# A list scheduler that follows two DMA rings, and packed attention scores unpacked by one wide and two corner masks

## The chip, the cores and the metric

The kernel runs on one NeuronCore of a Trainium2 chip. A core has a matrix engine (TensorE, "PE" in the profile; its weight loads are a row of their own, "PEld"), a vector engine (VectorE, "DVE"), an activation engine (ScalarE, "ACT"), GpSimd ("POOL") and SyncE ("SP"). Each engine runs its own instructions in their order and waits for the others through semaphores. Transfers are issued here from two queues, POOL's (loads, with a cast from float32 to bfloat16) and SP's (transposes and stores), and are carried by the core's 16 DMA engines. The metric is the device time of one execution in microseconds (us), less is better.

## The reference

Eight batches of eight heads, 576 positions, 64 numbers per head: sliding-window attention with a linear position bias, then a two-layer feed-forward network with squared ReLU on the 4608 tokens.

```python
scores = scale * np.matmul(q, k.transpose(0, 1, 3, 2))
rel = pos[:, None] - pos[None, :]
bias = slopes[:, None, None] * (-np.abs(rel).astype(np.float32))[None, :, :]
mask = (rel >= 0) & (rel < window)                 # window = 128
scores = np.where(mask, scores + bias[None], -1000000000.0)
attn = softmax(scores); attn_out = np.matmul(attn, v)
x = attn_out.transpose(0, 2, 1, 3).reshape(4608, 512)
out = np.maximum(x @ w_in, 0.0) ** 2 @ w_out       # w_in 512x2048, w_out 2048x512
```

## The kernel before

**Attention.** A batch is cut into five blocks of queries: four of 128 and one of 64, so there are 40 blocks, numbered m = 0 to 39 (called b0, b1 and so on in the order of loads). A block sees its own keys and those of the block before it. `load_block` loads k, q and v of a block; `turn` transposes k and q into `kqT`, on TensorE for the blocks of `KQ_PE`, else by a DMA transpose from SP (line 439); `score` issues the score matmuls; then come an exponential on ScalarE, a product on VectorE with a mask that holds bias and window, and in `mix` the product with v (line 612), whose extra column of ones gives the sum of the softmax, its reciprocal (635), the scaling (640), and the transpose of the result into `xT`, on TensorE for the blocks of `X_PE`, else by DMA (650).

**Packed scores.** From block 6 on, a whole block that is not the first of its batch is handled in "quarters". For a pair of heads the unpacked score row has 256 columns: 128 queries against the block's own keys, then the same 128 queries against the keys of the block before. Of those the lower 64 key rows can be non-zero in columns 0 to 191 only, and the upper 64 in columns 64 to 255 only. So the 64x64 parts of the array write 192 columns for each half of the keys (line 521), packed to the front of the bank; one exponential of 128x384 (two heads' pairs) reads them into `raw`, and two products of 64x384 (line 569, one for each half of the keys, because their columns start at different places) spread them into `Pq`. There are 21 such blocks, with four exponentials and eight products each. Score matmuls of three half blocks go out as one burst (`UNITS`), 48 matmuls where all are packed. Other blocks (line 530, 584, 591) are not packed; a 64-row block and the first block of the next batch form a pair.

**Feed-forward.** Tokens go in nine groups of 512 (g0 to g8). `fc_step` (line 716) makes 128 of the 2048 inner features for a group, `relu` and `square` follow on ScalarE (725) and VectorE (732), and `t_part` (778) multiplies four of 16 feature blocks into an output tile of 128 tokens. The group g+1 of the first layer is interleaved with the group g of the second. Group 0 is done in two halves of 256 tokens, group 1 in three parts (`SPLIT`). The weights come in four loads each, i0 to i3 (`w_in`) and o0 to o3 (`w_out`), between the first blocks, in the order of `FIRST`.

**Order.** `Plan` is a list scheduler that runs when the kernel is built. Every piece of work is a task with costs in ns per engine it may use, dependencies, buffers to take and to give back, and a key. `order` repeatedly takes the task that can start first; between tasks that can start at the same time the key decides. The key of attention work is a due time (`where`), less `AHEAD` or `LEAD`. The order that comes out is what the engines execute: a task whose data are later than planned holds up all that is behind it on its engine. A transfer is modelled by one number, `dma_free`: transfers go one after another, each with its own cost, whichever queue issued them. At most eight transfers are outstanding on a queue (`lanes`). `fill` puts matmuls on zeros ("filler", line 818) into planned gaps of TensorE before 26 us, and `warm` puts some at the very start.

Of the kernel before, what the change touches and what calls it, by code (L numbers as in the profile page):

```python
# [11 lines left out]
ALU = mybir.AluOpType  # L12
# [26 lines left out]
class Plan:  # L39


    LAT = {"PE": 260.0, "ACT": 220.0, "DVE": 220.0, "POOL": 200.0, "SP": 2200.0}
    BEGIN = {"POOL": 1260.0}

    def __init__(self, bufs, pools, cold, share):
        self.tasks = []
        self.bufs = bufs
        self.pools, self.cold, self.share = pools, cold, share
        self.bursts = []
        self.dma_free = 0.0  # L50

# [25 lines left out]

    def order(self):
        used = {tag: [] for tag in self.bufs}
# [17 lines left out]
        def avail(t):  # L97
            at = t.ready
            if t.dma is not None or t.engs.get("SP"):
                e = next(iter(t.engs))  # L100
                if len(lanes[e]) >= 8:
                    at = max(at, lanes[e][-8])
            more = {}
            for s in t.acq:
                if s.idx is not None:
                    continue
                more[s.tag] = more.get(s.tag, 0) + 1
                if s.tag in held:
                    if s.ffn:
                        at = self.ration(t, at, held[s.tag], left, used, free)  # L110
                        if at is None:
                            return None
                    free_at = sorted(0.0 if x is None else x.freed for x in held[s.tag] if x is None or not x.left)
                    if len(free_at) < more[s.tag]:
                        return None
                    at = max(at, free_at[more[s.tag] - 1])
                    continue
                u = used[s.tag]
                n = self.bufs[s.tag]
                i = len(u) + more[s.tag] - 1 - n  # L120
                if i >= 0:
                    old = u[i]
                    if old.left:
                        return None
                    at = max(at, old.freed)
            return at

        self.used = used
        done = []
        n_all = len(self.tasks)  # L130
        while len(done) < n_all:
            best = None
            for e, c in cand.items():
# [12 lines left out]
                if lo is not None and (best is None or lo[0][0] < best[0]):  # L146
                    best = (lo[0][0], e, lo[1])
            if best is None:
                raise RuntimeError("plan is stuck: " + repr([
# [7 lines left out]
            if t.dma is not None:  # L157
                at = max(st + dur + 900.0, self.dma_free)
                self.dma_free = at + t.dma
                t.end = self.dma_free + 900.0  # L160
                lanes[e].append(t.end)
            else:
                t.end = st + dur + (self.LAT[e] if t.lat is None else t.lat)
                if e == "SP":
                    lanes[e].append(t.end)
            free[e] = st + dur
            for x in t.engs:
                cand[x].remove(t)
            for s in t.acq:
# [11 lines left out]
                u.append(s)  # L181
            for s in t.rel:
                s.left -= 1
                s.freed = max(s.freed, t.end)
            for u in t.users:
                left[u] -= 1
                u.ready = max(u.ready, st + dur if e == "PE" and "PE" in u.engs else t.end)
                if not left[u]:
                    for x in u.engs:
                        cand[x].append(u)  # L190
            done.append(t)
# [5 lines left out]
def kernel(  # L197
# [17 lines left out]

    FIRST = "b0 b1 b2 b3 i0 i1 i2 o0 b4 b5 i3 o1 b6 b7 o2 b8 o3 b9"
    SPLIT = {0: [(0, 256), (256, 512)], 1: [(0, 192), (192, 320), (320, 512)]}
    EARLY = 0
    AHEAD = {10: -30, 1: 30, 4: 60, 9: -60, 5: 60, 0: 0, 12: 60, 11: 0, 2: -60, 8: -30, 7: 90, 6: 0, 3: 30, 24: 0, 14: 60, 18: 30, 25: 30, 23: 30, 16: -30, 13: 90, 21: 0, 19: 30, 17: 0, 22: 0, 20: 60, 15: 30}
    LEAD = 40  # L220

    KQ_PE = [0, 1, 2, 3, 4, 5, 6, 7, 8]
    X_PE = [0, 1, 2, 3, 4, 5, 6, 7, 8, 12, 17]
    WARM = 28
    FILL, UNTIL = 0.4, 26e3
    COLD = 12000
    QUARTERS = 6
    V0 = 1
    SHARE, SOON = 3, 500
    LONG, UNITS = 5, 3  # L230
    W_IN = [0, 4, 8, 12, 16]
    PAIR_AFTER, PAIR_KEY = 2, -140
    BANKS = {"A": 8}
# [21 lines left out]

    size = {"kq": 7, "v": 7, "kqT": 5, "P": 2, "x": 4, "Pq": 2, "raw": 2}
    kq = ring("kq", size["kq"], [128, 2, d_model])
    vt = ring("vt", size["v"], [128, H, D + 1])
    kqT = ring("kqT", size["kqT"], [128, 2 * C, 128])
    Pt = {nm: ring(nm, size[nm], [128, H, 2, 128]) for nm in ("P", "Pq")}  # L260
    raw = ring("raw", size["raw"], [128, H, 192])
    xt = ring("x", size["x"], [128, d_model])
# [92 lines left out]

    def load(key, ns, emit, deps=(), acq=()):
        return plan.add({"POOL": 900.0}, key, emit, deps, acq, dma=ns)

# [3 lines left out]
    def load_w_in(n, key):  # L362
        lo, hi = 128 * W_IN[n], 128 * W_IN[n + 1]

        def emit():
            nc.gpsimd.dma_start(w_in_sb[:, :, lo:hi], moe_w_in[:, lo:hi].rearrange("(c p) f -> p c f", p=128))  # L366
        t = load(key, {256: 1400.0, 512: 2550.0}[hi - lo], emit)
        t_win[W_IN[n]:W_IN[n + 1]] = [t] * (W_IN[n + 1] - W_IN[n])

    def load_w_out(n, key):  # L370
        def emit():
            nc.gpsimd.dma_start(
                w_out_sb[:, 4 * n:4 * n + 4, :],
                moe_w_out[n * 512:(n + 1) * 512, :].rearrange("(c p) f -> p c f", p=128))
        t_wout[n] = load(key, 2550.0, emit)

    s_in, t_in = {}, {}

    def load_block(m, key):
# [5 lines left out]
        for i, (nm, src) in enumerate((("k", k), ("q", q), ("v", v))):  # L385
            sl = s_in[m, nm]
            if wide and nm != "v":
                def emit32(i=i, src=src):
                    nc.sync.dma_start(kq32[:, i].rearrange("s (h d) -> s h d", h=H),
                                      src[b, :, kb * 128:kb * 128 + n, :].rearrange("h s d -> s h d"))  # L390
                t_in[m, nm] = plan.add({"SP": 450.0}, key + 0.01 * i, emit32, dma=870.0)
                continue
# [36 lines left out]
    def turn(m):  # L429
# [7 lines left out]
        if kq_by_dma:  # L437
            def turn_kq():
                nc.sync.dma_start_transpose(kqT[sk.idx], kq[s_in[m, "k"].idx].rearrange("s t f -> s (t f)"))
            t_kq = [plan.add({"SP": 1300.0}, due - 80, turn_kq, [t_in[m, "k"], t_in[m, "q"]], [sk],  # L440
                             [s_in[m, "k"]], dma=1300.0)]
        elif m == 0:
# [58 lines left out]
    def score(units):  # L501
# [8 lines left out]
        def burst():  # L510
            for sl in slots.values():
                bank(sl)
            for (ms, sP, work_of, _), j in units:
                for c in (2 * j, 2 * j + 1) if sP.tag == "Pq" else ():
                    m = ms[0]
                    for part, k0, q0, q1 in ((1, 0, 0, 128), (1, 64, 64, 128), (0, 64, 0, 128), (0, 0, 0, 64)):
                        mk = m - 1 + part
                        lo = (c % 2) * 256 + at_of[m, part] + q0 - k0
                        for half in range(2):
# [5 lines left out]
                for c in () if sP.tag == "Pq" else (2 * j, 2 * j + 1):  # L525
                    for m, mk, w, at, _ in work_of:
# [13 lines left out]
                      [x for u in units if u[1] == 1 for w in u[0][2] for x in w[4]])  # L540
        tm.n = 4 * sum(4 if u[0][1].tag == "Pq" else len(u[0][2]) * 128 // tall for u in units)
        plan.bursts.append(tm)
        chain["s"] = [tm]
        for (ms, sP, work_of, due), j in units:
# [6 lines left out]
            def view(t, pair=pair, lo=lo, hi=hi, n=n):  # L551
                if pair:
                    return t
                return t.rearrange("p c (t q) -> p c t q", t=2)[:, :, lo:hi, 0:n]

            for i in (2 * j, 2 * j + 1) if sP.tag == "Pq" else ():
                slot = slots[ms[0], i]
# [4 lines left out]
                def expo(i=i, slot=slot, sr=sr):  # L562
                    nc.scalar.activation(raw[sr.idx][:, 2 * i:2 * i + 2],  # L563
                                         slot.tile.rearrange("p (c x) -> p c x", c=2)[:, :, 0:192],
                                         AF.Exp, bias=0.0, scale=scale)
                te = plan.add({"ACT": act(384) + 50.0}, due - 28 + 3 * i, expo, [tm], [sr] if i == 0 else [], [slot])
                for k0 in (0, 64):
                    def mask(i=i, k0=k0, sr=sr, sP=sP):
                        nc.vector.tensor_tensor(  # L569
                            Pt["Pq"][sP.idx].rearrange("p h t q -> p h (t q)")[k0:k0 + 64, 2 * i:2 * i + 2, k0:k0 + 192],  # L570
                            raw[sr.idx][k0:k0 + 64, 2 * i:2 * i + 2],
                            masks.rearrange("p h t q -> p h (t q)")[k0:k0 + 64, 2 * i:2 * i + 2, k0:k0 + 192],
                            op=ALU.mult)
                    P_of[ms[0]][1].append(plan.add(
                        {"DVE": dve(384, 2)}, due - 28 + 3 * i, mask, [te] + t_zero_P + t_mask,
                        [sP] if i == 0 and k0 == 0 else [], [sr] if i == 3 and k0 else []))
            for i in () if sP.tag == "Pq" else (2 * j, 2 * j + 1):
# [18 lines left out]
    def mix(m):  # L596
# [51 lines left out]
        if x_by_dma:  # L648
            def turn_x():
                nc.sync.dma_start_transpose(xT[:, :, t0:t0 + n], xt[sx.idx][0:n, :])  # L650
            t_xT[b, kb] = plan.add({"SP": 1280.0}, due, turn_x, t_norm, [], [sx], dma=800.0)
        else:
# [16 lines left out]
    m = 0  # L669
# [72 lines left out]
    def store_tile(g, t, slot, lo, hi, last, key, engs):  # L742
# [17 lines left out]
        while held and max(held[0][0], HOLD + held[0][0] // 2) <= n or n >= NG * 4 - 4 and held:  # L760
            n0, k0, st, so0 = held.pop(0)
            if NG * 4 - 4 - odd <= n0 < NG * 4 - 4:
                plan.add({"POOL": 900.0}, k0, lambda st=st: st(nc.gpsimd), [te, evacs[n0]], [], [so0], dma=650.0)
            else:
                plan.add({"SP": 350.0}, k0, lambda st=st: st(nc.sync), [te, evacs[n0]], [], [so0])

# [74 lines left out]

    done = fill(plan.order())
    with tc.manual_schedule():
# [32 lines left out]
```

## Time and profile before

| | |
|---|---|
| median of 4 runs | 313.68 us (311.76 to 314.73) |
| the profiled execution | 314.73 us, of which 313.0 us span from first to last instruction |
| granted TensorE clock | 0.995 |
| TensorE busy | 298.1 us, 95% |
| VectorE, ScalarE busy | 184.0 us, 171.9 us |
| packed mask products (line 569) | 168 of 64x384, mean 351 ns |
| loads from POOL's queue | 84.6% of the 16 DMA engines' span |
| transfers of SP's queue | 40.9% of the same |

The profile was taken on one execution, the slowest of the four. The times of single instructions in it run from the start to the end of the instruction; neighbours on one engine overlap, so that the pace of a row of equal instructions can be faster than their mean time. The shares of the two DMA queues add up to more than 100% because packets of both queues are in the DMA engines together.

### The profile page before, as it was taken

How to read it: one execution, taken by the hardware profiler on the slowest of the kernel's cores; microseconds unless marked ns; L12 is line 12 of the kernel's file. 1: busy time of each engine (PE TensorE's matmuls, PEld its weight loads, DVE VectorE, ACT ScalarE, POOL GpSimd, SP SyncE). 2: the span in 40 equal slices, each digit the busy share in tenths (PEclk: the TensorE clock that was granted, in tenths of full speed). 3: DMA queues.
4: the chain of work that ended last, by engine and by line, in shares of the span. 5: the costliest groups of instructions: out<-in, count | busy, mean ns of one | idle time of the engine just before them, and what ended most of it. 6: DMA issues, size and time to landing. Idle time of an engine off the chain costs nothing.

```text
span 313.0 us, 7797 instructions
## 1 busy us (share of the span) xinstructions
PE 298.1 (95%) x3080; PEld 168.9 (54%) x3123; DVE 184.0 (59%) x563; ACT 171.9 (55%) x339; POOL 107.3 (34%) x134
## 2 busy tenths in 40 slices
PE   8779999999989989999999999999999999999996
PEld 4557877776454555554545544554454544444443
DVE  7656768858469597875785853773587522222200
ACT  4775876575157764665665744664565443434411
POOL 8936678546465365274175040100000000000000
PEclk9899999999999999999999999999999999999999
DMA  9999999999999999999999999995312310000022
GB/s 132 144 202 178 173 184 130 129 129 139 141 150 147 132 156 153 129 127 151 151 186 186 180 144 223 222 144 135 112 54 69 101 44 36 34 34 34 36 90 78
DMA packets 168629, 40.04 MB, mean 128 GB/s; under 512 B 159952, under 2 KB 164304, under 8 KB 168592
## 3 DMA queue, kind: packets, MB, share of 16 engines
q0 software_dynamic: 114896, 18.88, 84.6%
q1 hardware_dynamic: 53696, 20.65, 40.9%
q8 instruction: 24, 0.39, 0.5%
q14 instruction: 13, 0.11, 0.1%
HBM read 36.70 MB, written 9.44 MB: 147 GB/s over the span
## 4 chain that ended last, share of the span: by engine, by line
PE 83%; DMA 8%; POOL 4%; DVE 2%; issue 2%; ACT 1%; POOLq 0%; ACTq 0%
PE A L716 37%; PE A L778 35%; PE A L612 5%; DMA w_out_sb<-in_moe_w_out_dram 5%; DMA kqT<-kq 4%; PE A L521 3%; POOL kq L397 2%; DVE Pq L569 2%; PE A L530 1%; POOL vt L397 1%; ACT raw L563 1%; POOL w_in_sb L366 1%; PE A L467 1%; PE A L658 0%; DVE x L640 0%
## 5 line engine op out<-in xcount | busy, mean ns | idle before, releaser
L716 PE MATMUL A<-xT,w_in_sb 128*128 128x512 bf16 (+3 forms) x759 | 148.2, 325 | 2.7 <-DMA w_in_sb<-in_moe_w_in_dram 1.9
L778 PE MATMUL A<-w_out_sb,g 128*128 128x512 bf16 (+2 forms) x558 | 142.2, 373 | 2.9 <-issue 2.1
L725 ACT ACTIVATE rt<-A 128x512 bf16<-128x512 f32 (+1 forms) x148 | 86.2, 591 | 96.3 <-PE A L716 73.2
L732 DVE TENSOR_TENSOR g<-rt 128x512 bf16<-128x512 bf16 (+1 forms) x148 | 60.7, 413 | 76.5 <-ACT rt L725 76.0
L716 PEld LDWEIGHTS <-w_in_sb 128*128 128x128 bf16 x768 | 68.5, 98 | 53.8 <-DMA w_in_sb<-in_moe_w_in_dram 2.6
L778 PEld LDWEIGHTS <-g 128*128 128x128 bf16 x592 | 54.1, 98 | 54.4 <-issue 0.3
L569 DVE TENSOR_TENSOR Pq<-raw,masks 64x384 bf16<-64x384 bf16 x168 | 59.0, 351 | 9.6 <-ACT raw L563 6.4
L397 POOL DMA_DIRECT2D kq<-in_k_dram x39 | 33.6, 860 | 45.8 <-DMA kqT<-kq 24.1
L397 POOL DMA_DIRECT2D vt<-in_v_dram x40 | 34.1, 857 | 41.5 <-PE A L612 26.5
L397 POOL DMA_DIRECT2D kq<-in_q_dram x39 | 33.5, 860 | 14.9 <-DMA kq<-in_q_dram 5.6
L563 ACT ACTIVATE raw<-A 128x384 bf16<-128x384 f32 x84 | 35.6, 500 | 5.1 <-PE A L521 4.6
L748 ACT ACTIVATE osb<-A 128x512 f32<-128x512 f32 (+1 forms) x36 | 21.5, 597 | 23.5 <-PE A L778 22.9
L640 DVE TENSOR_TENSOR x<-A,rec 128x256 bf16<-128x256 f32 (+1 forms) x80 | 32.0, 415 | 0.8
L756 POOL DMA_DIRECT2D out_dram<-osb x3 | 1.7, 563 | 84.4 <-ACT osb L748 84.4
L584 ACT ACTIVATE P<-A 128x512 bf16<-128x512 f32 (+1 forms) x48 | 23.6, 579 | 4.0 <-PE A L530 3.9
L635 DVE RECIPROCAL rec<-A 128x4 f32<-128x4 f32 (+1 forms) x80 | 13.2, 174 | 16.7 <-PE A L612 15.9
L612 PEld LDWEIGHTS <-Pq 128*128 128x128 bf16 x336 | 15.5, 97 | 10.1 <-DVE Pq L569 1.1
L612 PE MATMUL A<-vt,Pq 128*128 128x65 bf16 x336 | 17.5, 193 | 1.8 <-DVE x L640 1.0
L612 PEld LDWEIGHTS <-P 128*128 128x128 bf16 x240 | 11.5, 100 | 4.3
L591 DVE TENSOR_TENSOR P<-P,pair_masks 128x512 bf16<-128x512 bf16 x28 | 11.6, 421 | 2.9 <-ACT P L584 2.2
L612 PE MATMUL A<-vt,P 128*128 128x65 bf16 x240 | 12.6, 197 | 0.2 <-issue 0.2
L521 PEld LDWEIGHTS <-kqT 64*64 64x64 bf16 x672 | 8.5, 108 | 5.8 <-issue 5.8
(43 smaller groups left out, 110.6 us busy)
## 6 DMA issues: line engine op xcount, KB each, us to landing
out_dram<-osb SPq DMA_DIRECT2D x32, 256.0 KB, 2.7
vt<-in_v_dram POOLq DMA_DIRECT2D x32, 128.0 KB, 10.2
kq<-in_k_dram POOLq DMA_DIRECT2D x31, 128.0 KB, 10.7
kq<-in_q_dram POOLq DMA_DIRECT2D x31, 128.0 KB, 11.1
w_in_sb<-in_moe_w_in_dram POOLq DMA_DIRECT2D x4, 512.0 KB, 9.6
w_out_sb<-in_moe_w_out_dram POOLq DMA_DIRECT2D x4, 512.0 KB, 9.6
out_dram<-osb POOLq DMA_DIRECT2D x3, 256.0 KB, 2.3
kq<-in_k_dram POOLq DMA_DIRECT2D x8, 64.0 KB, 12.2
```

What stands on the lines that cost most here:

```text
L397: nc.gpsimd.dma_start(o, src[b, :, kb * 128:kb * 128 + n, :].rearrange("h s d -> s h d"))
L521: nc.tensor.matmul(slots[m, 2 * j + half].tile[k0:k0 + 64, lo:lo + q1 - q0], kqT[sk_of[mk].idx][rows, c, k0:k0 + 64], kqT[sk_of[m].idx][ro ...
L563: nc.scalar.activation(raw[sr.idx][:, 2 * i:2 * i + 2], slot.tile.rearrange("p (c x) -> p c x", c=2)[:, :, 0:192], AF.Exp, bias=0.0, scale ...
L569: nc.vector.tensor_tensor(Pt["Pq"][sP.idx].rearrange("p h t q -> p h (t q)")[k0:k0 + 64, 2 * i:2 * i + 2, k0:k0 + 192], raw[sr.idx][k0:k0 ...
L584: nc.scalar.activation(Pv(i), view(slot.tile.rearrange("p (c x) -> p c x", c=2)), AF.Exp, bias=0.0, scale=scale)
L612: nc.tensor.matmul(bank(slot_v)[:, hi * (D + 1):(hi + 1) * (D + 1)], Pt[sP.tag][sP.idx][:, place(h)].rearrange("p t q -> p (t q)")[:, at_o ...
L640: nc.vector.tensor_tensor(xt[sx.idx][0:n, hf * 256:(hf + 1) * 256].rearrange("p (h e) -> p h e", h=4), pv[0:n, :, 0:D], srec.tile[0:n, :]. ...
L716: nc.tensor.matmul(bank(slot)[:, fi * w:(fi + 1) * w], w_in_sb[:, cc, fc * 128:(fc + 1) * 128], xT[:, cc, g * 512 + lo:g * 512 + hi], star ...
L725: nc.scalar.activation(srt.tile[:, 0:cols], slot.tile[:, 0:cols], AF.Relu, bias=0.0, scale=1.0)
L732: nc.vector.tensor_tensor(sg.tile[:, fcs[0]:fcs[-1] + 1, lo:hi], r, r, op=ALU.mult)
L748: nc.scalar.activation(so.tile[:, lo:hi], slot.tile[:, lo:hi], AF.Copy)
L778: nc.tensor.matmul(bank(slot)[:, lo:hi], sg.tile[:, fc, t * 128:(t + 1) * 128], w_out_sb[:, fc, lo:hi], start=fc == 0, stop=fc == FCB - 1)
```

## The change

The planner gets a model of the two rings of transfers. An issued transfer enters its ring after a set time, is served at a rate that it shares with the other ring in the proportion of a weight per kind (a fifth number of a transfer: 13.6 for block loads, 80 for weights and stores, about 27 for transposes), and lands a further set time later; transposes and stores are put later while POOL's ring has work. The fetching of TensorE instructions (every 128) takes time off POOL's ring. The landing is put `MARGIN` = 500 ns later still. Tasks now become ready at events, in the order of time.

The packed score layout is altered so that all 128 key rows share one wide product: packed columns 0 to 127 hold the unpacked columns 64 to 191 for both halves of the keys, and columns 128 to 191 hold the corner of each half (unpacked 0 to 63 of the lower, 192 to 255 of the upper). Each exponential is followed by one product of 128 rows by two times 128 columns; after every second exponential two corner products of 64 rows by four times 64 columns follow. The score matmuls of the lower keys against the block's own queries are split in two, so a pair of heads takes ten matmuls in place of eight. `raw` is allotted 256 columns per head in place of 192, and the rings `kq` and `v` have six buffers in place of seven.

Constants of the order are set anew: the order of first loads, the due times, which blocks' results are transposed on TensorE (block 10 in place of block 17), warm-up, filler, and where the masks of the pairs are built.

```diff
+    RING = {"w": (1400.0, 1000.0), "t": (50.0, 450.0), "c": (500.0, 350.0), "f": (670.0, 1400.0)}
-        self.dma_free = 0.0
...
+        def share():
+            a, b = rings["SP"], rings["POOL"]
+            if a and b:
+                x, y = a[0][1], b[0][1]
+                return {"SP": x / (x + y), "POOL": y / (x + y)}
+            return {"SP": 1.0, "POOL": 1.0}
...
+                if e is not None:
+                    t = rings[e].pop(0)[2]
+                    late = self.RING[t.dma[0]][1] + (2200.0 if t.dma[0] in "tc" and rings["POOL"] else 0.0)
+                    heapq.heappush(events, (now + late + margin, t.seq, 1, t))
...
-                at = max(st + dur + 900.0, self.dma_free)
-                self.dma_free = at + t.dma
-                t.end = self.dma_free + 900.0
-                lanes[e].append(t.end)
+                lanes[e].append(t)
+                late = self.RING[t.dma[0]][0] + (2600.0 if t.dma[0] in "tc" and rings["POOL"] else 0.0)
+                heapq.heappush(events, (st + dur + late, t.seq, 0, t))
...
+            if e == "PE":
+                if (fetched + t.n) // 128 > fetched // 128 and rings["POOL"] and st < 150e3:
+                    advance(max(now, st))
+                    rings["POOL"][0][0] += 900.0 if st < 25e3 else 400.0
+                fetched += t.n
...
-    FIRST = "b0 b1 b2 b3 i0 i1 i2 o0 b4 b5 i3 o1 b6 b7 o2 b8 o3 b9"
+    FIRST = "b0 b1 b2 b3 i0 i1 o0 b4 i2 b5 i3 o1 b6 b7 o2 b8 o3 b9"
-    EARLY = 0
-    AHEAD = {10: -30, 1: 30, 4: 60, 9: -60, 5: 60, 0: 0, ...}
-    LEAD = 40
+    EARLY = -60
+    AHEAD = {10: -60, 1: 0, 4: 90, 9: 90, 5: -30, 0: -60, ...}
+    LEAD = 0
-    X_PE = [0, 1, 2, 3, 4, 5, 6, 7, 8, 12, 17]
-    WARM = 28
-    FILL, UNTIL = 0.4, 26e3
+    X_PE = [0, 1, 2, 3, 4, 5, 6, 7, 8, 10, 12]
+    WARM = 20
+    FILL, UNTIL = 0.9, 26e3
-    V0 = 1
-    SHARE, SOON = 3, 500
+    V0 = 2
+    SHARE, SOON = 3, 1000
+    MARGIN = 500
-    PAIR_AFTER, PAIR_KEY = 2, -140
+    PAIR_AFTER, PAIR_KEY = 1, -100
-    size = {"kq": 7, "v": 7, "kqT": 5, "P": 2, "x": 4, "Pq": 2, "raw": 2}
+    size = {"kq": 6, "v": 6, "kqT": 5, "P": 2, "x": 4, "Pq": 2, "raw": 2}
-    raw = ring("raw", size["raw"], [128, H, 192])
+    raw = ring("raw", size["raw"], [128, H, 256])
...
-                    for part, k0, q0, q1 in ((1, 0, 0, 128), (1, 64, 64, 128), (0, 64, 0, 128), (0, 0, 0, 64)):
+                    for part, k0, q0, q1, lo in ((0, 64, 0, 128, 64), (1, 0, 0, 64, 128), (1, 0, 64, 128, 0),
+                                                 (1, 64, 64, 128, 0), (0, 0, 0, 64, 64)):
                         mk = m - 1 + part
-                        lo = (c % 2) * 256 + at_of[m, part] + q0 - k0
+                        lo += (c % 2) * 256
...
-                for k0 in (0, 64):
-                    def mask(i=i, k0=k0, sr=sr, sP=sP):
+                whole, low, high = slice(0, 128), slice(0, 64), slice(64, 128)
+                cuts = [(whole, slice(2 * i, 2 * i + 2), whole, slice(64, 192))]
+                if i % 2:
+                    four, corner = slice(2 * i - 2, 2 * i + 2), slice(128, 192)
+                    cuts += [(low, four, corner, low), (high, four, corner, slice(192, 256))]
+                for n, w in enumerate(cuts):
                     P_of[ms[0]][1].append(plan.add(
-                        {"DVE": dve(384, 2)}, due - 28 + 3 * i, mask, [te] + t_zero_P + t_mask,
-                        [sP] if i == 0 and k0 == 0 else [], [sr] if i == 3 and k0 else []))
+                        {"DVE": dve(256, 2)}, due - 28 + 3 * i, functools.partial(mask, *w),
+                        t_exp[-1:] + t_exp[-2:-1] * (n > 0) + t_zero_P + t_mask,
+                        [sP] if i == 0 else [], [sr]))
```

## The prediction, made before the changed kernel was run

> **What bounds the kernel now.** I read the busy row first, then the stages, then who TensorE waits for, then the two kinds of work that the change edits. The busy row, and the stages (columns: stage, its length, then busy us and count for each engine, granted clock, DMA engines' share where both queues count, GB/s):
>
> ```profile
> PE 298.1 (95%) x3080; PEld 168.9 (54%) x3123; DVE 184.0 (59%) x563; ACT 171.9 (55%) x339; POOL 107.3 (34%) x134
> ...
> 0.00:30.00 30.00, 24.33 (x247) 17.54 (x249) 19.05 (x66) 18.92 (x41) 20.59 (x30) 0.94 1.59 163
> 30.00:60.00 30.00, 29.11 (x447) 23.90 (x451) 23.34 (x73) 20.77 (x44) 22.14 (x27) 1.00 1.91 158
> 60.00:90.00 30.00, 28.37 (x390) 18.24 (x395) 19.09 (x60) 15.48 (x33) 14.73 (x19) 1.00 1.87 137
> 90.00:120.00 30.00, 28.52 (x386) 15.78 (x391) 24.15 (x79) 18.17 (x36) 16.56 (x20) 1.00 1.85 146
> 120.00:200.00 80.00, 78.57 (x839) 40.10 (x851) 53.56 (x161) 47.95 (x94) 30.07 (x36) 1.00 1.82 166
> 200.00:296.00 96.00, 95.10 (x701) 46.18 (x711) 44.06 (x126) 47.68 (x89) 2.70 (x4) 1.00 0.30 76
> ```
>
> TensorE is idle for 5.7 us of the first 30, for 0.9 + 1.6 + 1.5 = 4.0 between 30 and 120, and for 2.3 in the 176 us after that. So the only gains are idle time ahead of 120 us; elsewhere the time is matmuls, which the change doesn't remove. Who ended the waits of TensorE, from 30 us on:
>
> ```profile
> PE A L778 <- issue: 2.1, 13, 0.2
> PE A L612 <- DVE x L640: 1.0, 1, 1.0
> PE A L530 <- DMA kqT<-kq: 0.8, 1, 0.8
> PE A L612 <- DVE Pq L569: 0.7, 3, 0.3
> ```
>
> The 13 short ones stand behind score bursts, where the array goes from 64x64 parts back to the whole; they stay. The other three rows, 2.5 us, are work that came later than planned. A wait also empties the pipeline: the one of 0.26 before 49.12 us lies between matmul starts at 48.67 and 49.12 that would be 29 ns apart, so 0.42 is lost. With 0.15 more for each of the five, about 3.2 us could be had after 30 us.
>
> **Score bursts: 168 more matmuls and weight loads.** One burst of before, and one with pairs in it:
>
> ```profile
> 43.33 0.24 PE L521 MATMUL A<-kqT 64*64 64x128 bf16 x4
> 43.39 0.22 PE L521 MATMUL A<-kqT,kqT 64*64 64x128 bf16 x4
> 43.44 0.22 PE L521 MATMUL A<-kqT 64*64 64x128 bf16 x4
> ...
> 112.44 0.20 PE L530 MATMUL A<-kqT,kqT 64*64 64x64 bf16 x4
> 112.47 0.26 PE L530 MATMUL A<-kqT 64*64 64x64 bf16 x8
> 112.56 0.20 PE L530 MATMUL A<-kqT,kqT 64*64 64x64 bf16 x4
> ```
>
> Eight packed matmuls (two heads) start every 88 ns: rows 43.39 to 43.48 in the trace; four quarters of the array work side by side, each with one of 128 columns (about 59 ns) and one of 64 (about 29). The change cuts the 128 of the two lower-key quarters into two of 64: 3 x 29 = 87 ns beside 59 + 29 = 88 in the upper ones. In the pair rows each quarter does 64, 64 and 128 columns in 0.12 us, so two short ones in a row do keep 29 to 31 ns. A rule speaks against this: the Trainium skill, "TensorE: Matmul & The Clock Gate", section "Wait — 56ns, not 53.3ns?", says that starts never come closer than about 25 ns. By the rule 168 x 25 = 4.2 us more; by the row, where 48 matmuls start in 0.52 us (11 ns each), at most 2 ns per pair of heads, 84 x 2 = 0.2 us. I go by the row. Upper end: the extra step is not hidden behind the other quarters, 84 x 29 = 2.4 us. A gain is excluded, since the upper quarters stream the same columns. Taken: +0.2.
>
> **Masks: 168 products of 384 become 84 + 84 of 256 elements.** Rows with the nearest shapes (shape and count, busy us, mean ns), and runs of neighbours (start, length, count):
>
> ```profile
> L569 DVE TENSOR_TENSOR Pq<-raw,masks 64x384 bf16<-64x384 bf16 x168 | 59.0, 351 | 9.6 <-ACT raw L563 6.4 <-PE A L612 0.2
> L591 DVE TENSOR_TENSOR P<-P,masks 128x256 bf16<-128x256 bf16 x8 | 2.1, 284 | 1.0 <-ACT P L584 1.0
> ...
> 86.98 2.97 DVE L569 TENSOR_TENSOR Pq<-raw,masks 64x384 bf16<-64x384 bf16 x8 [3.86 <-ACT raw L563]
> 17.58 1.42 DVE L591 TENSOR_TENSOR P<-P,masks 128x512 bf16<-128x512 bf16 x4
> ```
>
> By mean times a block falls from 8 x 351 to 8 x 284 ns, 0.54 us; over 21 blocks 11.3 us of VectorE. But the pace differs: eight of 384 columns take (2.97 - 0.35) / 7 = 0.374 us each, more than the (1.42 - 0.42) / 3 = 0.333 of the larger 512. The Trainium skill, "VectorE: DVE Perf Modes", section "Two Vector instructions with no wait between them", gives a reason: an instruction that starts in another group of 32 partitions than the one before is held until all earlier ones have ended. Before, every product alternates between partitions 0 and 64; after, only the high corner and its follower do, four of eight. A pace of 256 columns without hold is 0.333 less half of 512 columns at (421 - 284) / 256 ns each (421 is the mean of the 512 row), 0.196; with hold 0.28. So a block takes 4 x 0.196 + 4 x 0.28 = 1.9 us in place of 8 x 0.374 = 3.0: 1.1 us, 23 us over all. VectorE is 59% busy, so nothing of this is on the path directly; what lies on it is the three waits on Pq. The planner had these products at 384 / 2 / 0.96 + 72 = 272 ns, against 374 real: for a full burst of 12 it was 1.2 us too early. For 256 it says 205, near 196 to 280. I take the three waits as gone: part of the next sum. If it is not so, they cost the 0.7 + 3 x 0.15 = 1.15 us that they cost now. The corners wait for two exponentials, but the second half of them was the last to come before too.
>
> **The two rings.** SP's transposes take a median 9.5 us from issue to landing and up to 12.4, and the chain has one of 11.09 us from 76.33 that ends in TensorE's 0.8 us wait. The old planner gives it its own 1.3 us in one line of transfers. A planner that puts transposes later while POOL's ring is full will place the bursts later and fill with feed-forward work, of which there is plenty. Of the 3.2 us I take 2.2; all (3.2) is one end, and nothing, or new waits of the same size (+3), the other, since the due times are new as well. SP's own queue keeps the same counts (31 and 29 transposes): block 10's goes, block 17's comes, four transposes of 56 ns on TensorE each, net 0. The changed keys decide only between tasks that can start together; no row prices them: 0, inside those ends.
>
> **Six buffers in place of seven.** POOL, where all later loads queue behind a waiting one, waits for kq to be freed only from about 120 us on (24 us in all). Before, its waits are for older loads to land, the limit of eight. With one buffer less the trace would hold loads of blocks 24 to 28 by 1 to 4 us; block 27's q lands at 129.2 and its transpose is issued at 137.1, so 8 us of slack hides that. Taken: 0. Gone beyond 8 us of delay; then each us is one of TensorE's.
>
> **The opening.** The first weight wait is data: i0 and i1 land at 18.39 and 22.04 us, and TensorE waits for both:
>
> ```profile
> 18.44 0.83 PE L716 MATMUL A<-xT,w_in_sb 128*128 128x256 bf16 x6 [0.65 <-DMA w_in_sb<-in_moe_w_in_dram]
> 22.08 1.05 PE L716 MATMUL A<-xT,w_in_sb 128*128 128x256 bf16 x8 [1.24 <-DMA w_in_sb<-in_moe_w_in_dram]
> ...
> 26.35 0.61 PE L658 MATMUL A<-ident,x 128*128 128x128 bf16 x8
> 27.16 1.24 PE L778 MATMUL A<-w_out_sb,g 128*128 128x512 bf16 x4
> ```
>
> With o0 and b4 ahead of i2, o0 lands at about 24.6 in place of 27.12 and i2 at about 29.1 in place of 24.55 (o0 took 2.57, b4 2.02 behind it). From 22.04 to 29.1 TensorE needs 7.1 us of other work. There is: i1 on the first half, 16 x 0.109 = 1.75 us; i0 and i1 on the second half, 3.5; o0 on four tiles, 16 x 0.216 = 3.5; the rest of blocks 2 and 3 with their transposes, about 1.4. Together 10, but 3.5 + 1.75 of it need blocks 2 and 3 turned, which the trace has at 26.35, held there by the order, not by their loads (14.94). So i2 is covered if they are turned by about 26.5. What can be gained: the second wait in part, 0.5 us of filler and waits at 24.3 and 26.8, and the clock (mean 0.94 in the first 30 us; more filler keeps it up), against fillers that hold up data that come early. I take -1.5; ends -2.5 and +4.6 (i2's whole delay).
>
> **The sum,** against the profiled execution: span 313.0 + 0.2 - 2.2 - 1.5 = 309.5, with the 1.7 around it 311.2, that is 3.5 less than 314.73. The median of the runs is 313.68, so about 310.0.
>
> **Rivals.** (1) The waits are only moved: the same 5 to 9 us of idle time elsewhere, since an order with new keys meets other late data. For it: a single execution varied by 3 us; against: VectorE's plan error does go. Sum 0.2 with nothing gained: 313.9. (2) Slower: i2. If blocks 2 and 3 are still turned at 26.35 or later, TensorE has only 1.75 + 1.4 + two tiles of o0, 1.7, from 22.04 on, stands from about 26.9 to 29.1, and starts the second half behind i2; 2.2 to 4.6 us with nothing gained after, so 316.1 to 318.5, near 317.3. It decides from the point where their transposes end after 26.5. (3) Slower: with later due times in all blocks (`LEAD` 40 to 0) a transpose of 11 to 12 us meets its burst in the 30 to 120 us stage in more than one place: one wait of 0.8 to 1 for each of some four, 317.
>
> **Chances and numbers.** The forecast, 308 to 312.3: 0.64. Rival 1: 0.15. Rival 2: 0.12. Rival 3: 0.09. 1% is 3.1 us, about what a measurement of this kernel can tell from no change: below 310.5 lies two thirds of the forecast and a little besides, 0.45; above 316.8 most of rivals 2 and 3 and the unhidden burst, 0.21; between, 0.34. Range: from all 3.2 and 2.5 us gained (308.2, rounded down for the spread) to the middle of the slower rivals.
>
> **What would show it.** A burst of 60 matmuls should last as long as 48 did, with starts within 0.53 us. The packed products should show 284 ns means and a pace of about 0.24. Waits of line 612 on Pq should be gone; those on kqT too. Between 22 and 29 us TensorE should run the second half of group 0 and line 778, with no wait over 0.5 us. Idle time in the stages to 120 us should fall from 9.7 to about 6. Wrong if the bursts grow by 0.15 us or more, if i2 is waited for, or if a new wait for a transfer stands in the 30 to 120 us stage.

## The result, and the profile after

The changed kernel takes 312.5 us (median of 43 runs, 310.74 to 314.98), the kernel before 313.65 us (median of 64). The ratio is 0.9969 with a 95% interval of 0.9958 to 0.998: 0.3% faster, a quarter of the 1.2% that was forecast. Ratios, here and below, are of fast runs alone (a run more than 1.5% above the fastest of its kernel is left out), so they are not exactly the quotients of the medians. The profiled execution took 313.26 us with a span of 311.5; that of before 314.73 and 313.0.

The busy row of the page after, then its stages to 120 us (columns as in the prediction):

```profile
PE 299.4 (96%) x3264; PEld 169.5 (54%) x3306; DVE 170.3 (55%) x563; ACT 171.4 (55%) x338; POOL 107.4 (34%) x134
...
0.00:30.00 30.00, 26.09 (x275) 18.28 (x277) 19.90 (x67) 19.47 (x41) 21.69 (x31) 1.00 1.59 165
30.00:60.00 30.00, 29.32 (x481) 24.21 (x485) 22.56 (x77) 20.68 (x44) 21.29 (x26) 1.00 1.91 160
60.00:90.00 30.00, 29.47 (x429) 18.83 (x434) 17.23 (x62) 14.55 (x31) 14.84 (x18) 1.00 2.01 142
90.00:120.00 30.00, 27.98 (x381) 14.89 (x385) 21.09 (x74) 18.48 (x37) 14.18 (x18) 1.00 1.91 135
```

VectorE falls by 13.7 us, where 11.3 by mean times and 23 by pace were worked out, and TensorE is idle for 7.1 us to 120 us in place of 9.7. But part of TensorE's busy time in the first 30 us is filler (30 matmuls on zeros, 15 before), and the stage from 90 to 120 us is worse than before. The waits of TensorE from 30 us on, after:

```profile
PE A L835 <- issue: 1.6, 10, 0.2
PE A L579 <- DMA kqT<-kq: 0.8, 1, 0.8
PE A L772 <- DMA xT<-x: 0.7, 1, 0.7
PE A L772 <- issue: 0.3, 2, 0.2
PE A L772 <- ACT raw L613: 0.2, 1, 0.2
PE A L668 <- DVE Pq L621: 0.2, 1, 0.2
```

The waits of the product with v (line 668 now) on Pq and on x went from 1.7 us to 0.2. Two waits for transposes are there, 0.8 us at 109 us and 0.7 us at 119 us.

Busy time can't tell work from filler, so I use a measure of my own from the trace: **lost time**, the elapsed time less the TensorE work done by then. Work is counted by weight loads, one for each matmul, because some matmul records are missing (3264 of 3306 are in this profile). It is the count of weight loads of each kind times the pace of that kind at full clock (216 ns for 512 columns, 163, 109, 83, 56 for 384, 256, 192, 128, 29 for the product with v, 11 for each score matmul, 9.7 in bursts with one cut); filler counts as lost. It was taken at 30, 120 and 280 us in every profile:

| kernel | lost by 30 us | 30 to 120 | 120 to 280 | this execution |
|---|---|---|---|---|
| before, first profile | 15.6 | 5.9 | 2.7 | 314.73 |
| before, second profile | 15.2 | 6.3 | 2.7 | 314.79 |
| four kernels with the old planner, below: e2, e5, e6, e7 | 14.6 to 15.4 | 4.8 to 5.1 | 2.7 | 313.5 to 313.6 |
| changed, first profile | 14.5 | 4.7 | 2.7 | 313.26 |
| changed, second profile | 13.3 | 3.5 | 2.7 | 310.91 |

Both profiles of before are executions about 1.1 us above its median, and the second of the changed kernel 1.6 below its own. The six profiles with the old planner have a mean of 15.1 and 5.3 (e13 and e17 below, slower than before, are not among them); the changed kernel's two have 13.9 and 4.1. That is 1.2 less in each of the two stages, and 0.8 is spent again in score bursts: about 1.6, of which some 0.4 is the luck of two executions whose mean lies that much under the median. 1.15 was measured. The two profiles of the changed kernel differ from each other by as much as 1.2, so they alone prove little; by the same measure the eight other profiles with the new planner and its due times (e1, e3, e4, e11, e12, e15, e16, e18) lose 13.5 to 14.9 by 30 us and 2.9 to 5.1 from 30 to 120.

### The profile page after: what moved, and what is told of

Same layout as the page of the kernel before. It is cut to its first block, busy times and chain, and to the rows that moved or that the text cites. A ratio compares the mean times of both kernels' runs of the same rounds, so it can differ in the third digit from the quotient of the medians.

```text
span 311.5 us, 8171 instructions
## 1 busy us (share of the span) xinstructions
PE 299.4 (96%) x3264; PEld 169.5 (54%) x3306; DVE 170.3 (55%) x563; ACT 171.4 (55%) x338; POOL 107.4 (34%) x134
## 4 chain that ended last, share of the span: by engine, by line
PE 81%; DMA 11%; POOL 4%; issue 2%; ACT 1%; DVE 1%; POOLq 0%; ACTq 0%
PE A L835 36%; PE A L772 35%; PE A L668 4%; DMA w_in_sb<-in_moe_w_in_dram 4%; DMA kqT<-kq 3%; DMA xT<-x 3%; PE A L570 3%; POOL kq L445 2%; PE A L579 1%; POOL vt L445 1%; PE A L714 1%; PE A L515 1%; POOL w_in_sb L414 0%; ACT P L640 0%; ACT rt L781 0%
## 5 line engine op out<-in xcount | busy, mean ns | idle before, releaser
L772 PE MATMUL A<-xT,w_in_sb 128*128 128x512 bf16 (+3 forms) x757 | 144.9, 325 | 2.2 <-DMA xT<-x 0.7
L621 DVE TENSOR_TENSOR Pq<-raw,masks 64x256 bf16<-64x256 bf16 (+1 forms) x168 | 43.4, 285 | 11.3 <-ACT raw L613 8.5
L668 PEld LDWEIGHTS <-Pq 128*128 128x128 bf16 x336 | 15.1, 97 | 8.2 <-DVE Pq L621 0.6
L668 PE MATMUL A<-vt,Pq 128*128 128x65 bf16 x336 | 16.6, 193 | 0.2 <-DVE Pq L621 0.2
L570 PEld LDWEIGHTS <-kqT 64*64 64x64 bf16 x840 | 9.7, 108 | 5.6 <-issue 5.5
```

What stands on the lines that cost most here:

```text
L570: nc.tensor.matmul(slots[m, 2 * j + half].tile[k0:k0 + 64, lo:lo + q1 - q0], kqT[sk_of[mk].idx][rows, c, k0:k0 + 64], kqT[sk_of[m].idx][ro ...
L621: nc.vector.tensor_tensor(P, raw[sr.idx][ks, hs, lo], masks.rearrange("p h t q -> p h (t q)")[ks, hs, to], op=ALU.mult)
L668: nc.tensor.matmul(bank(slot_v)[:, hi * (D + 1):(hi + 1) * (D + 1)], Pt[sP.tag][sP.idx][:, place(h)].rearrange("p t q -> p (t q)")[:, at_o ...
L772: nc.tensor.matmul(bank(slot)[:, fi * w:(fi + 1) * w], w_in_sb[:, cc, fc * 128:(fc + 1) * 128], xT[:, cc, g * 512 + lo:g * 512 + hi], star ...
```

## The experiments

Each ratio is to runs of the kernel before on the same chip, with its 95% interval. Two theories: A, the planner and the opening give the gain and the new layout costs a little; B, the shorter products give it.

**The two halves.** e1 puts the old layout back into the changed kernel, which keeps its six buffers; e2 puts the new layout alone into the kernel before, which keeps its seven.

```diff
e1, in the changed kernel:
-  for part, k0, q0, q1, lo in (... five matmuls ...)
+  for part, k0, q0, q1 in ((1, 0, 0, 128), (1, 64, 64, 128), (0, 64, 0, 128), (0, 0, 0, 64)):
-  cuts = [whole, low corner, high corner]     # 256 elements each
+  for k0 in (0, 64): mask(...)                # 64x384
e2: the same two edits the other way round, in the kernel before
```

> The changed kernel with the packed layout of before put back (eight score matmuls for two heads, eight products of 64x384 a block, raw of 192 columns); planner, order of loads, constants and six buffers stay changed. Theory A (the gain is the planner's and the opening's, the new layout costs 0.74 us in its bursts and its shorter products hide beside other work): 0.7 to 0.8 us under the changed kernel, about 311.8 us, ratio to before 0.994, with bursts of 48 matmuls back at 0.52 us from first to last start. Theory B (the shorter products give the gain, the planner's order alone gives none): about 313.7, ratio 1.000, with waits of the product with v on Pq of 0.7 us or more back in the profile.

> The kernel before with the new packed layout alone (ten score matmuls for two heads, one wide product after each exponential and two corners after each second one, planned at 205 ns); old planner, order of loads and constants, seven buffers. Theory A: the bursts' 0.74 us is paid and at most part of the 1.2 us of waits on Pq comes back: 313.6 to 314.4, ratio 1.000 to 1.0025. Theory B: the waits on Pq (0.7 us and 0.15 of refill for each) and some of x go, more than the bursts cost: 312.5 or less, ratio 0.997.

Measured: e1 0.9974 (0.9959 to 0.9988), 312.52 us; e2 1.0012 (0.9987 to 1.0036), 313.8 us. The plan with the old layout is as good as the whole change, and the new layout alone gives nothing. So A holds for the source of the gain, but not for its sum: e1 should have been 0.7 us under the changed kernel, and it wasn't. Its waits, from 30 us on:

```profile
PE A L660 <- DVE Pq L617: 1.0, 3, 0.4
PE A L660 <- DVE x L688: 0.2, 1, 0.2
```

The waits on Pq are back, 1.0 us in three. The new layout removes them and pays about as much in its bursts, as the next experiments show.

**The price of the cut.** e5 cuts one score matmul of the kernel before in two and leaves its plan and masks alone; e13 cuts both long ones. e4, and e12 once more, is a third layout in the changed kernel: the 64 shared columns of the previous block first, each half's own corner in the middle, the 64 shared ones of the own block last. Every score matmul is then contiguous, eight for two heads, with eight products of 256 elements a block as in the change; the output is the same. e6 is that layout in the kernel before.

```diff
e5, kernel before:
-  ((1, 0, 0, 128), (1, 64, 64, 128), (0, 64, 0, 128), (0, 0, 0, 64))
+  ((1, 0, 0, 64), (1, 0, 64, 128), (1, 64, 64, 128), (0, 64, 0, 128), (0, 0, 0, 64))
e13, kernel before:
+  ((1, 0, 0, 64), (1, 64, 64, 128), (1, 0, 64, 128), (0, 64, 0, 64), (0, 0, 0, 64), (0, 64, 64, 128))
e4 and e12, changed kernel:
-  ((0, 64, 0, 128, 64), (1, 0, 0, 64, 128), (1, 0, 64, 128, 0), (1, 64, 64, 128, 0), (0, 0, 0, 64, 64))
+  ((1, 0, 0, 128, 64), (1, 64, 64, 128, 128), (0, 64, 0, 128, 0), (0, 0, 0, 64, 0))
-  cuts = [(whole, slice(2 * i, 2 * i + 2), whole, slice(64, 192))]
...
+  cuts = [(whole, four, slice(0, 64), slice(128, 192)), (whole, four, slice(128, 192), slice(64, 128)),
+          (low, four, slice(64, 128), low), (high, four, slice(64, 128), slice(192, 256))] if i % 2 else []
```

> The kernel before with one edit: the score matmul of the lower keys against the own block's 128 queries is cut into two of 64 columns (ten matmuls for two heads), into the same columns of the bank; same plan, same order, same masks. If a burst is on the path in full: bursts from 0.52 to 0.57 or 0.58 us from first to last start, and 0.7 to 0.8 us more in all, 314.1 us, ratio 1.0024. If waits elsewhere swallow it: 313.4, ratio 1.000.

> The kernel before with both 128-column score matmuls of two heads cut into 64s: twelve matmuls in place of eight, 336 more with as many weight loads in all; each quarter of the array does three short ones, 94 ns by the pace of the cut kernel, so the bursts should last about as long as with one cut (0.56 to 0.58 us). If the array time is the price: like the kernel with one cut, 314.1 to 314.6, ratio 1.003 to 1.005. If instructions cost besides (fetching them): another 0.5 to 0.8 us, 315.0 or more, ratio 1.006 to 1.008.

> The changed kernel with a third packed layout: columns 0 to 63 hold what both halves of the keys share from the block before, 64 to 127 each half's own corner, 128 to 191 what both share from the own block. Every score matmul is contiguous again, eight for two heads in place of ten; eight products of 256 elements a block as in the changed kernel, but all four of a half block behind its second exponential. If the three short matmuls in a row in the lower quarters (31 ns each, 95 for two heads against 88) are the whole cost of the bursts and it is paid in full: bursts back to 0.52 us, 0.74 us less than the changed kernel, 311.8, ratio to before 0.994. If the time only turns into waiting for transfers: 312.5.

> The four-matmul layout in the changed kernel once more, beside the changed kernel on the same chip, since it had few undisturbed runs. If its gain is the bursts' price alone (0.75 us by their lengths in the profile): 0.75 us under the changed kernel. If what the cutting cost the kernel before (0.5%) is what the changed kernel pays too: 1.6 us under it, ratio to before 0.991 to 0.992.

> The kernel before with the third packed layout of the four-matmul experiment (eight contiguous score matmuls for two heads, eight products of 256 elements a block behind every second exponential); old planner, constants, seven buffers. If shorter products are worth something by themselves: the waits on Pq and x (1.7 us with 0.15 of refill each) go in part, 312.4 to 312.8, ratio 0.997 to 0.998. If the four-matmul version's gain belonged to the new plan alone: 313.4, ratio 1.000.

| kernel | ratio to before | interval | median, us |
|---|---|---|---|
| e5, one cut | 1.0051 | 1.0027 to 1.0075 | 314.52 |
| e13, both cut | 1.0075 | 1.0043 to 1.0107 | 315.69 |
| e6, third layout, old plan | 0.9986 | 0.9969 to 1.0003 | 313.25 |
| e4, third layout, new plan | 0.9914 | 0.9882 to 0.9947 | 310.71 |
| e12, the same again | 0.9924 | 0.9900 to 0.9948 | 310.95 |
| changed kernel again (e10, below), beside e12 | 0.9970 | 0.9947 to 0.9993 | 312.60 |

One cut costs the kernel before 0.5%, and going from the changed kernel to the third layout gains 0.5% twice (in six runs each time). Only e5 and e13 change nothing but the cut, with the same order and masks; the third layout also puts all four products of a half block behind its second exponential, and the planner makes a new order. The weight loads of a burst of three half blocks (start, length, count), in the kernel before, the changed one, e13 (two bursts) and e12:

```profile
43.33 0.58 PEld L521 LDWEIGHTS <-kqT 64*64 64x64 bf16 x48 [0.42 <-issue]
```

```profile
43.59 0.66 PEld L570 LDWEIGHTS <-kqT 64*64 64x64 bf16 x60 [0.42 <-issue]
```

```profile
42.71 0.67 PEld L521 LDWEIGHTS <-kqT 64*64 64x64 bf16 x72 [0.42 <-issue]
...
52.11 0.72 PEld L521 LDWEIGHTS <-kqT 64*64 64x64 bf16 x72 [0.42 <-issue]
```

```profile
43.19 0.58 PEld L570 LDWEIGHTS <-kqT 64*64 64x64 bf16 x48 [0.42 <-issue]
```

Sixty take 0.08 us longer than 48. From first to last matmul start, summed over the 18 bursts of three half blocks after 40 us (a step over 70 ns, a wait, counted as 70), it is 10.1 us before and in the third layout, 10.7 in e5, 11.0 in the changed kernel and 11.75 in e13. So 0.6 of e5's 1.1 us, 0.9 of the 1.65 between the changed kernel and e12, and 1.65 of e13's 2.1 are seen in the bursts; the three costs are differences of medians, and by the ratios they would be 1.6, 1.4 and 2.35. The rest is within what these intervals leave open; e13's second cut added 1.05 us in the bursts and about as much in the time (1.0 by the medians, 0.75 by the ratios), so there is no sign that the rest grows with the number of instructions. What it is isn't settled.

The shorter products are worth something only once the cut is gone, and with the new plan: e4 and e12 are 0.5 to 0.6% faster than e1 (same bursts, new plan), while e6 has gained 0.14%, with an interval that reaches past zero, on the old plan. The planner orders the work by the products' costs, so in e4 and e12 the products and the order that comes with them are measured together.

**The parts of the plan.** Constants and model, one at a time and in pairs, always with the old layout and seven buffers, in the kernel before.

```diff
e7:  opening's constants: FIRST, WARM 20, FILL 0.9, V0 2, PAIR_AFTER 1, PAIR_KEY -100
e8:  model of the two rings, MARGIN 500; all constants of before
e14: model and opening's constants
e15: model and due times: EARLY -60, AHEAD, LEAD 0, SOON 1000, block 10 for block 17 in X_PE
e17: EARLY -60 alone, old planner
```

> The kernel before with the opening's constants of the changed kernel alone: order of first loads, WARM 20, FILL 0.9, V0 2, PAIR_AFTER 1, PAIR_KEY -100; old planner, due times, layout, buffers. If the opening gives its 1.15 us: 312.3, ratio 0.9965. If its difference between the two profiles was one execution's: 313.4 and ratio 1.000.

> The kernel before with the planner of the changed kernel (two rings, instruction fetch, margin 500) and every constant of the order, the layout and the seven buffers of before. If the model of transfers gives the gain by itself: 312.5 or less, ratio 0.997, with no wait of TensorE for a transpose. If the gain needs the constants that were set with it: 313.4 or more.

> The kernel before with the new planner and the opening's constants (loads, warm-up, filler, v of block 0, place of the pair masks), but due times, TensorE transposes of results, layout and buffers of before. If the opening needs the model to be planned well: 312.6, ratio 0.997, lost time at 30 us 14.5 or less. If the due times are what counts: 313.4, ratio 1.000.

> The kernel before with the new planner and the due times set with it (EARLY, AHEAD, LEAD, SOON, block 10 in place of 17 on TensorE), but the opening's constants, layout and buffers of before. If due times and model belong together: 312.5 to 312.8, ratio 0.997 to 0.998, with less than 4.7 us lost from 30 to 120 us. If the opening is what counts: 313.4, ratio 1.000.

> The kernel before with EARLY = -60 in place of 0, nothing else: first-layer work of group 1 gets keys 60 lower, so that it may run while group 0 waits for weights. If this is the due time that fills the opening: 312.6, ratio 0.997, about 14.2 us lost by 30 us. If it is the others (due times of single blocks with the model of the rings): 313.4, ratio 1.000.

| kernel | ratio to before | interval |
|---|---|---|
| e7, opening's constants | 1.0002 | 0.9988 to 1.0016 |
| e8, model of the rings | 0.9995 | 0.9976 to 1.0014 |
| e14, model and opening | 1.0026 | 1.0007 to 1.0045 |
| e15, model and due times | 0.9964 | 0.9942 to 0.9986 |
| e17, EARLY alone | 1.0040 | 1.0019 to 1.0061 |

Model and due times together hold all of the gain; the model by itself gives none, and with the opening's constants it is 0.3% slower (e14). The waits in the profile of e8:

```profile
PE A L764 <- DMA xT<-x: 2.5, 1, 2.5
PE A L660 <- DVE Pq L617: 0.6, 3, 0.3
```

The wait of 2.5 us for a transpose is new, but that execution took 316.02 us, the slowest of the twelve and 2.55 above their median, so this wait is not shown to be the plan's; in e14, with the same due times, it is 0.3. The due times without the model can't be run: the old planner finds no order for them (every buffer of kqT ends up held by work that waits for another). So what the model adds to the due times is not known by itself. EARLY alone has its 14.0 us lost by 30 us, as expected of it, but 6.9 from 30 to 120, and is 0.4% slower.

**Single constants in the changed kernel, and the second look.** e3 puts i2 back before o0 and b4; e11 turns block 17 on TensorE and block 10 by DMA; e9 and e10 are the two kernels unchanged.

```diff
e3:
-  FIRST = "b0 b1 b2 b3 i0 i1 o0 b4 i2 b5 ..."
+  FIRST = "b0 b1 b2 b3 i0 i1 i2 o0 b4 b5 ..."
e11:
-  X_PE = [0, 1, 2, 3, 4, 5, 6, 7, 8, 10, 12]
+  X_PE = [0, 1, 2, 3, 4, 5, 6, 7, 8, 12, 17]
```

> The changed kernel with one constant set back, the order of the first loads (i2 before o0 and b4, as before). If that order made the opening's 1.15 us: about 313.6, the lost time at 30 us back from 14.5 to about 15.6, and a wait of over 1 us for a weight load between 20 and 28 us. If it was the early attention work (warm clock, v of block 0 later, filler): 312.5 to 312.8, lost time at 30 us near 14.5.

> The changed kernel with one constant set back: the result of block 17 is turned on TensorE and that of block 10 by DMA, as before. Theory A (the new wait of 0.7 us at 119 us is block 17's DMA transpose, 9.1 us from issue to landing, which the kernel before did in four matmuls): 0.5 to 0.9 us less than the changed kernel beside it, no wait for xT there. Rival (another transpose becomes the late one, or the due times were set to this choice): equal to it or slower, a wait for xT or kqT elsewhere in 80 to 125 us.

> The kernel before, unchanged, for a second profile of it. Time lost on TensorE (elapsed less the work done at the full pace of each kind of matmul) by 30 us between 14.5 and 15.7, and 4.8 to 5.9 more from 30 to 120 us. If it lies at 14.2 or less at 30 us, the opening's difference between the first two profiles was one execution's.

> The changed kernel, unchanged, beside the two that follow. 312.3, ratio to before 0.9965; in the profile 13.5 to 14.6 us lost by 30 us and 3.7 to 4.8 more from 30 to 120, the waits for transposes of blocks 17 and 19 at 109 and 119 us again.

e3: 0.9978 (0.9956 to 1.0), 312.77 us, 14.0 us lost by 30 us: the order of loads makes no difference that these runs can tell. e11: 1.0008 (0.9981 to 1.0035), 313.04 us: not faster but perhaps slower than e10 beside it, so my theory of block 17 fell. e9's lost time lies as expected in the opening (15.2) and 0.4 above it from 30 to 120 us (6.3); at 314.79 us it lies again above the median. The second profile of the changed kernel has neither of the two waits for transposes. Its waits from 30 us on that are 0.2 us or more:

```profile
PE A L579 <- issue: 0.3, 1, 0.3
PE A L772 <- issue: 0.2, 1, 0.2
PE A L668 <- DVE Pq L621: 0.2, 1, 0.2
```

The 0.8 and 0.7 us for transposes in its first profile were that execution's own.

**Towards a better version.** e16 widens the margin of the third layout's plan; e18 gives it the opening's constants of before.

```diff
e16, in e4:  MARGIN = 1000 in place of 500
e18, in e4:  FIRST, WARM 28, FILL 0.4, V0 1, PAIR_AFTER 2, PAIR_KEY -140
```

> The four-matmul version with every landing planned 1000 ns late in place of 500. If late transfers still cost it: 310.5 or less, ratio to before 0.990. If what is left is not late transfers, but single waits of 0.3 to 1.2 us that no transfer explains: 311.0 or more, ratio 0.992 or above, since the order changes without need.

> The four-matmul version with the opening's constants of before (order of loads, warm-up 28, filler 0.4, v of block 0, place of the pair masks), and the new planner and due times. If those constants do nothing: 310.8, ratio 0.992. If they belong to the new plan: 311.5 or more.

e16: 0.9929 (0.9906 to 0.9951), 310.8 us; e18: 0.9926 (0.9903 to 0.9949), 310.95 us. Neither differs from e4 and e12. The third layout in the changed kernel, 310.7 to 310.95 us, is 0.5% under the changed kernel and 0.8% under the one before, and is faster than both.

## Why the prediction was wrong

The direction was right, and VectorE did shed its work; the size was not. Two terms of the sum failed. The bursts, put at +0.2 us, cost 1.1 us by the medians and 1.6 by the ratio where nothing but the cut was made (e5), and 1.65 between the changed kernel and e12; that is shown by runs. The savings, put at -3.7, were worked out on an execution 1.05 us above the median and then taken from the median; that this failed is read from profiles. By its own steps:

- **The sum against one execution.** I worked out 3.7 us of savings from the waits of an execution of 314.73 us, and took the net 3.5 from the median of 313.68 (which makes 310.2, not the 310.0 that I wrote). The 1.05 us between the two seems to be part of the same idle time: the four old-planner profiles of 313.5 to 313.6 us have 4.8 to 5.1 us lost from 30 to 120 us, not 5.9, and 14.6 to 15.4 in the opening, not 15.6. What one execution loses above the median can't be saved from the median. No run tests this, but the sum agrees: e12, without the cut, is 2.65 us under the kernel before, which is the 3.7 less 1.05; with the cut's 1.65 added, 1.0 is left, and 1.0 is what the changed kernel gained beside it. That the figures meet so closely is luck, since each difference is uncertain by some 0.7 us.
- **Bursts, +0.2.** 0.8 to 0.9 in the changed kernel's bursts, 1.1 to 1.65 in time. I counted 3 x 29 ns for the lower quarters, while the pair rows that I quoted said 29 to 31; three short ones in a row take 31.5 each, so two heads start every 95 ns and not every 88, as in these rows of e13:

```profile
42.77 0.23 PE L521 MATMUL A<-kqT,kqT 64*64 64x64 bf16 x6
42.83 0.23 PE L521 MATMUL A<-kqT 64*64 64x64 bf16 x6
42.87 0.23 PE L521 MATMUL A<-kqT,kqT 64*64 64x64 bf16 x6
```

  That makes 0.6 us over the 84 pairs of heads. My sign of being wrong, 0.15 us a burst, was too coarse: 0.05 us in each of 18 bursts is already 0.9. The row was still the better guide: the rule of about 25 ns between starts, which the prediction cites, would have given 4.2, and starts in a burst were 8 to 11 ns apart on average.
- **Masks.** VectorE fell from 184.0 to 170.3 us, and ten products of the new kind run at a pace of 0.27 us, against 0.24 forecast. In the trace the starts of this row lie 201 to 210 ns apart where the next product starts at the same partition, and 289 to 321 where it does not (after the first pair, 381 apart); 196 and 280 were forecast. The row after, start, length and count:

```profile
44.54 2.71 DVE L621 TENSOR_TENSOR Pq<-raw,masks 128x256 bf16<-128x256 bf16 x10 [0.83 <-ACT raw L613]
```

  The waits on Pq are nearly gone. To put this into the 2.2 us of the rings was a mistake of bookkeeping: with the new plan it is worth 0.5% by itself, and the cut took it back.
- **Rings, -2.2.** 1.2 by the profiles, the model alone nothing (e8). Nor were the bursts put later where the waits had been: up to 147 us they start at most 0.6 us later than before, or earlier, and only from 160 us on are they 5 to 8 us later. The weight loads of the seventh burst after 40 us, before and after:

```profile
107.22 0.58 PEld L521 LDWEIGHTS <-kqT 64*64 64x64 bf16 x48 [0.42 <-issue]
...
102.71 0.65 PEld L570 LDWEIGHTS <-kqT 64*64 64x64 bf16 x60 [0.42 <-issue]
```

  The gain took due times set against the model (e15).
- **The opening, -1.5.** 1.2 by the profiles, but not through o0 and b4, filler or warm-up, which change nothing that these runs can tell (e3, e7, e18). The lost time of 14.1 in e15, 14.0 in e17 and 14.3 in e18, all with the old opening, says that the due times did it, on one profile each. The clock did rise as forecast, but no gain is seen from it. In e7 the granted clock of the first 30 us is 1.00 in place of 0.94, and 15.1 us are lost all the same, with new waits of 1.5 us for o0 and 1.2 for v; e18 has 0.89 there and is as fast as e12 with 1.00. The first 30 us of e7 and of e18, columns as above:

```profile
0.00:30.00 30.00, 24.49 (x262) 17.29 (x263) 19.40 (x68) 19.12 (x40) 22.46 (x32) 1.00 1.59 164
...
0.00:30.00 30.00, 25.27 (x270) 19.19 (x271) 20.38 (x69) 20.41 (x42) 20.72 (x30) 0.89 1.60 166
```

- **Six buffers and i2.** Nothing seen: e15 with seven buffers gains as much as the changed kernel with six. Rival 2 needed the transposes of block 3 after 26.5 us, and they are done at 23; i2 was waited for 0.4 us at 28.3.
- **Rivals.** Rival 1, waits only moved, comes nearest to the number (313.9), but by these runs it is not what happened: there were two gains, from the due times and from the shorter products, and one cost, the cut.

## What to carry to other kernels

A sum of waits needs the typical execution, so ask first how far the profiled one lies from the median and take that difference out of what can be saved. When a layout is changed for one engine, look for the version that leaves the other engine's instructions as they were: here the same masks were to be had without the cut matmul. A better model of transfers in the planner was worth nothing here until the due times were set against it again.

## What the runs showed of the hardware that was not expected

A 64x64 quarter of the array takes 28 to 29 ns for a 64-column matmul with its own weights when it alternates with one of 128 columns (the kernel before), and 31.5 when three follow each other (e13), with the other three quarters at work beside it. In e13, with 72 matmuls and 72 weight loads in a burst, the starts spread over 0.58 to 0.69 us, more than three times 31.5 for each of six pairs of heads (0.57) would need; 144 instructions in 0.633 us are 4.4 ns each.

The short waits named "issue" behind bursts (13 in the first profile of before) are gaps in the record. They stand in the six profiles that have 42 or 43 fewer matmul records than weight loads (3080 and 3123 in the first profile of before), and are absent from the 14 that have as many of one as of the other (3306 and 3306 in the second profile of the changed kernel), whose bursts have the same length. So the 2.3 us of idle time after 120 us that I read as TensorE's were not idle. Eight profiles (e2, e3, e4, e10, e11, e12, e13, e18) have one wait named "issue" of 0.3 to 1.3 us between 58 and 114 us, four of them within a score burst. No run here shows what they wait for.
